# A memory-bound decode kernel: V of quad 14 in halves, a new order of the last V and wo, W_down in 128, 120 and 96 rows, fewer VectorE instructions, and 16 small loads of x

## The chip, the cores and the metric

The kernel runs on one core of a Trainium2 chip. The metric is the device time of one execution in microseconds (us). "Span" is the time from the first to the last instruction in the profile; it is about 2 us shorter than the time.

Names used below: the work on the K and V caches is done in 16 "quads" (0 to 15). A quad is four heads of one batch row: 8.39 MB of K and as many of V. "K15" is the K of quad 15, "V14" the V of quad 14. A load is spread over up to 16 DMA engines. The trace's landing records give the time at which each of them signalled that its share had landed; "the slowest engine" is the last of them, "the fastest" the first.

## The reference

The reference is a decode step: layer norm, attention over a cache of 8192 positions (2 batch rows, 32 heads of 128), a gated MLP, and two residuals.

```python
# A_x (2,1,512); k_cache, v_cache (2,32,8192,128); wq (512,4096); wo (4096,512)
# W_gate, W_up (512,1376); W_down (1376,512); all bf16
q = layernorm(x) @ wq
p = softmax(q @ k_cache^T * 128**-0.5)
h = x + (p @ v_cache) @ wo
n = layernorm(h)
gate = n @ W_gate;  gate = gate * (gate > 0)
out = h + (gate * (n @ W_up)) @ W_down
```

K and V together are 268 MB. Everything else is small beside that.

## The kernel before

K lands in a ring of two buffers, V in one buffer. VectorE multiplies K by q and folds it to scores, ScalarE takes the exponential, TensorE multiplies by V. All large loads are issued by SyncE (SP), in one order.

```python
    kring = ctx.enter_context(tc.tile_pool(name="kring", bufs=2))
    vring = ctx.enter_context(tc.tile_pool(name="vring", bufs=1))
# ... cut
    def lanes_of(o):
        osb = opool.tile([P, Dh], f32, tag="row", name="osb")
        nc.vector.tensor_scalar_mul(osb, o[:, 0:Dh], turn_of[:, 0:1])
        for t in range(1, TG):
            nc.vector.scalar_tensor_tensor(out=osb, in0=o[:, t * Dh:(t + 1) * Dh],
                                           scalar=turn_of[:, t:t + 1], in1=osb,
                                           op0=ALU.mult, op1=ALU.add)
        return osb
# ... cut
    for n in range(N - 1):                      # N = 16 quads
        scores(n, HALVES if n == 0 else (0, T))
        if n + 2 < N:
            load_k(n + 2)
        gather()
        collect()                               # lanes_of for a finished pair of quads
        if n + 2 < N:
            weighted_v(n)
            load_v(n + 1)                       # the single V buffer is free again
# ... cut
    load_wo(0)
    L = N - 1
    vts[L] = vts[L - 1]
    weighted_v(L - 1, 0, T // 2)
    load_part(vts[L], A_v_cache, L, 0, T // 2)
    weighted_v(L - 1, T // 2, T)
    CUTS = (T // 2, T * 7 // 8, T)
    for lo, hi in zip(CUTS[:-1], CUTS[1:]):
        load_part(vts[L], A_v_cache, L, lo, hi)
    for k in range(1, NGR):
        load_wo(k)
    scores(L)
# ... cut: W_gate and W_up are loaded, then W_down in 128, 128 and 88 rows of 4 KB
    attention_rows(0, NK - JG)                  # the wo rows that need no V15
    for lo, hi in zip(CUTS[:-1], CUTS[1:]):
        weighted_v(L, lo, hi)                   # second half of V15
    collect()
    gather()
    normalize(B - 1, NGR - 1)
    attention_rows(NK - JG, NK)                 # the last wo rows
# ... cut: layer norm, MLP, store
```

The softmax here doesn't subtract the row's maximum and nothing guards it: scores larger than these inputs give would overflow.

Of the kernel before, what the change touches and what calls it, by code (L numbers as in the profile page):

```python
# [7 lines left out]
ACT = mybir.ActivationFunctionType  # L8
ALU = mybir.AluOpType
AXIS = mybir.AxisListType  # L10


def _view(t, offset, dims):
    return bass.AP(tensor=t.tensor, offset=t.offset + offset, ap=[t.ap[0]] + list(dims))
# [3 lines left out]
def kernel(  # L18
# [13 lines left out]
    nc = tc.nc  # L32
    P = nc.NUM_PARTITIONS
    B, Sq, D = A_x.shape
    _, Hkv, Sk, Dh = A_k_cache.shape
    Hq = A_wq.shape[1] // Dh
    F = B_W_gate.shape[1]
# [37 lines left out]
    NG = T // TG  # L75
    pm = consts.tile([P, R + NG * W2], bf16)
    row_of = consts.tile([P, Q], f32)
    nc.vector.memset(eps_t, EPS)
    nc.vector.memset(mean_c, 1.0 / D)
    nc.vector.memset(zm, 0.0)  # L80
    nc.vector.memset(row_of, 0.0)
    ident = consts.tile([P, P], bf16)
    masks.make_identity(nc, ident)
    nc.gpsimd.memset(pm, 0.0)
# [11 lines left out]
    def build_masks():  # L96
        def red(out, in_, axis=AXIS.X):
            nc.vector.tensor_reduce(out=out, in_=in_, axis=axis, op=ALU.add)

        red(turn_of, ident.rearrange("p (g t h) -> p t g h", t=TG, h=G), AXIS.XY)  # L100
        red(lane_of, ident.rearrange("p (g u t h) -> p u h g t", u=2, t=TG, h=G), AXIS.XY)
        red(head_blk, ident.rearrange("p (h m) -> p h m", h=G))
        red(row_of[:, 0:B], ident.rearrange("p (g q) -> p q g", q=Q)[:, 0:B, :])
        red(pick, ident.rearrange("p (h m) -> p m h", m=M4))
        nc.vector.tensor_copy(spread, _view(lane_of, 0, [[G, 2], [1, G], [0, M4]]))
        nc.vector.tensor_copy(same, _view(head_blk, 0, [[0, NS], [1, G], [0, M4]]))

    ctx.enter_context(tc.manual_schedule(engines={ENG.PE, ENG.DVE, ENG.Activation, ENG.SP}))

# [31 lines left out]
    for c in range(KC):  # L141
# [6 lines left out]
    rstd = misc.tile([P, B], f32)  # L148
    nc.scalar.activation(out=rstd, in_=variance(xd, "ln1"), func=ACT.Sqrt, bias=eps_t, scale=1.0)
    nc.vector.reciprocal(out=rstd, in_=rstd)  # L150
    xn = misc.tile([P, KC, B], bf16)
    nc.vector.tensor_tensor(out=xn, in0=xd, in1=rstd.unsqueeze(1).to_broadcast([P, KC, B]),
                            op=ALU.mult)
    xnb = opool.tile([P, KC, B, Q], bf16, tag="row")
    nc.vector.tensor_copy(xnb, xn.unsqueeze(3).to_broadcast([P, KC, B, Q]))
    nc.scalar.activation(out=warm, in_=xn[0:1, 0, 0:1], func=ACT.Exp)
    build_masks()


# [39 lines left out]
    def load_v(n, cuts=(0, T)):  # L199
        vts[n] = vring.tile([P, T, Dh], bf16, tag="v", name="v")  # L200
        for lo, hi in zip(cuts[:-1], cuts[1:]):
            load_part(vts[n], A_v_cache, n, lo, hi)
# [4 lines left out]
    def scores(n, cuts=(0, T)):  # L207

        b, i = seq[n]
        kt = kts[n]  # L210
        sc = spool.tile([P, T], f32, tag="sc", name="sc")
        for lo, hi in zip(cuts[:-1], cuts[1:]):
            kp = kt[:, lo:hi, :]
            nc.vector.tensor_tensor(out=kp, in0=kp,  # L214
                                    in1=_view(qrep[:, b, i, :], 0, [[0, hi - lo], [1, Dh]]),
                                    op=ALU.mult)
            width = Dh
            while width > 8:
                half = width // 2
                nc.vector.tensor_tensor(out=kp[:, :, 0:half], in0=kp[:, :, 0:half],  # L220
                                        in1=kp[:, :, half:width], op=ALU.add)
                width = half
            nc.vector.tensor_reduce(out=sc[:, lo:hi], in_=kp[:, :, 0:8], axis=AXIS.X, op=ALU.add)  # L223
        for h in range(G):
            ps = slice(h * Q, (h + 1) * Q)
            nc.scalar.activation(out=p_of[ps, :, :, h],  # L226
                                 in_=sc[ps, :].rearrange("p (g t) -> p g t", t=TG), func=ACT.Exp,
                                 accum_out=zm[ps, b, i:i + 1],
                                 scale=SCALE)
# [19 lines left out]

    def lanes_of(o):  # L250

        osb = opool.tile([P, Dh], f32, tag="row", name="osb")
        nc.vector.tensor_scalar_mul(osb, o[:, 0:Dh], turn_of[:, 0:1])  # L253
        for t in range(1, TG):
            nc.vector.scalar_tensor_tensor(out=osb, in0=o[:, t * Dh:(t + 1) * Dh],  # L255
                                           scalar=turn_of[:, t:t + 1], in1=osb,
                                           op0=ALU.mult, op1=ALU.add)
        return osb

    def lane(n):  # L260
# [51 lines left out]
    def normalize(b, k):  # L312
        g = b * NGR + k
        nc.vector.tensor_scalar_mul(oc[:, k * JG:(k + 1) * JG, b], ou[:, b, k], zi[:, g:g + 1])

    HALVES = (0, T // 2, T)
    load_k(0, HALVES)
    load_k(1)
    load_v(0)
    for n in range(N - 1):  # L320
        scores(n, HALVES if n == 0 else (0, T))
        if n + 2 < N:
            load_k(n + 2)
        gather()
        collect()
        if n + 2 < N:
            weighted_v(n)
            load_v(n + 1)


    W = kring.tile([P, RING], bf16, tag="k", name="W")
# [5 lines left out]
            out=wo_sb[:, k * JG:(k + 1) * JG, :].rearrange("p k n -> p (k n)"),  # L337
            in_=A_wo[r0:r0 + NS * G * Dh, :].rearrange("(p j) n -> p (j n)", p=P))

    load_wo(0)  # L340
    L = N - 1
    vts[L] = vts[L - 1]
    weighted_v(L - 1, 0, T // 2)
    load_part(vts[L], A_v_cache, L, 0, T // 2)
    weighted_v(L - 1, T // 2, T)
    CUTS = (T // 2, T * 7 // 8, T)
    for lo, hi in zip(CUTS[:-1], CUTS[1:]):
        load_part(vts[L], A_v_cache, L, lo, hi)
    for k in range(1, NGR):
        load_wo(k)  # L350

    scores(L)
# [4 lines left out]
    RD = 4  # L357
    MT = RD * P
    FT = (F + MT - 1) // MT
    offs = [min(j * MT, F - MT) for j in range(FT)]  # L360
    wd_sb = X[:, 2 * KC * F:2 * KC * F + FT * RD * D].rearrange("p (j r n) -> p j r n", r=RD, n=D)
    skip = ((FT - 1) * MT - offs[-1]) // RD
    assert F % RD == 0 and F >= MT
    if skip:
        nc.gpsimd.memset(wd_sb[0:skip, FT - 1], 0.0)  # L365
    for g, w, c0, c1 in ((0, B_W_gate, 0, KC), (1, B_W_up, 0, KC - 1), (1, B_W_up, KC - 1, KC)):
        nc.sync.dma_start(out=wgu[:, g, c0:c1].rearrange("p c n -> p (c n)"),
                          in_=w.rearrange("(p c) n -> p (c n)", c=KC)[:, c0 * F:c1 * F])
    for j in range(FT):
        p0 = skip if j == FT - 1 else 0  # L370
        rows = B_W_down[j * MT:min((j + 1) * MT, F), :].rearrange("(p r) n -> p r n", r=RD)
        for r0, r1 in ((0, RD),) if j < FT - 1 else ((0, RD - 1), (RD - 1, RD)):
            nc.sync.dma_start(out=wd_sb[p0:, j, r0:r1], in_=rows[:, r0:r1])

    invert_z()
    weighted_v(L, 0, CUTS[0])
    for b in range(B):
        normalize(b, 0)
        if b < B - 1:
            for k in range(1, NGR):  # L380
                normalize(b, k)

    ar_ps = ps_mm.tile([P, D], f32, tag="mm")
    nc.tensor.matmul(out=ar_ps, lhsT=ident[0:B, :], rhs=x_row, start=True, stop=False,
# [6 lines left out]
                             start=False, stop=(k + P // Q >= NK), skip_group_check=True)  # L391

    attention_rows(0, NK - JG)
    for lo, hi in zip(CUTS[:-1], CUTS[1:]):
        weighted_v(L, lo, hi)
    collect()
    gather()
# [6 lines left out]
    for c in range(KC):  # L404
        nc.tensor.matmul(out=h_ps[:, c, :], lhsT=ar.rearrange("p (m c) -> p c m", c=KC)[:, c, :],  # L405
                         rhs=row_of[:, 0:B], start=(c == 0), stop=True, skip_group_check=True)
    hc = misc.tile([P, KC, B], f32)
    nc.vector.tensor_copy(hc, h_ps)  # L408
    mu = centred(hc, "ln2")
    NR = Q // B  # L410
    hd = opool.tile([P, KC, NR, B], bf16, tag="hd")
    nc.vector.tensor_tensor(out=hd, in0=_view(hc, 0, [[B, KC], [0, NR], [1, B]]),
# [92 lines left out]
```

## Time and profile before

| | before |
|---|---|
| time, median of 3 runs (range) | 663.25 us (662.31 to 663.41) |
| span of the profiled execution | 661.5 us |
| SP's DMA queue, share of 16 engines' span | 98.7% |
| VectorE busy | 604.7 us (91%) |

The first fence has lines of the profile page of before: its head, the busy time of each engine, the rows of DMA busy share and of GB/s in 40 equal slices of the span, the queue of the SP loads (packets, MB, and the time that they took as a share of 16 engines' span), and the sums of the chain of work that ended last.

```profile
span 661.5 us, 2931 instructions
...
PE 117.5 (18%) x1211; PEld 51.3 (8%) x1211; DVE 604.7 (91%) x188; ACT 55.8 (8%) x142; POOL 4.3 (1%) x8
...
DMA  9999999999999999999999999999999999999896
GB/s 381 444 444 444 429 396 444 440 440 441 440 396 440 440 437 444 436 404 441 432 440 444 436 409 440 432 436 444 433 416 440 428 433 444 440 416 440 356 426 242
...
q1 hardware_dynamic: 6398, 281.06, 98.7%
...
DMA 75%; PE 15%; another core or an unknown queue 8%; DVE 1%; ACT 0%; issue 0%; SPq 0%; DVEq 0%
```

The DMA row is at 9 (90% busy or more) until three slices before the end, and the chain that ended last is DMA for 75% of the span. This kernel is bound by the stream of K and V. In the trace's landing records, each 8.39 MB K or V lands 19.36 us after the one before it, which is 433 GB/s. VectorE at 91% is close behind, but a line of the list of waits (what waits for what: idle time in all, count, longest) shows that it waits for K, 13.7 us in all, so it does not set the pace:

```profile
DVE k L214 <- DMA k<-in_A_k_cache_dram: 13.7, 10, 2.3
```

The next fence has the first line of SyncE's own waits: what released an issue, the idle time in all, how often, and the longest. It is the wait of one load for an earlier one; the lines after it are waits for VectorE and TensorE to free a buffer.

```profile
SPq L192 <- DMA v<-in_A_v_cache_dram: 286.6, 15, 21.3
```

SP waits all the time, and that is harmless: when it ends, the engines still have an earlier load to work on. The next fence shows that for the end of the stream. It is the timeline of SP: start, duration, what was issued.

```profile
582.02 0.33 SPq L192 DMA_DIRECT2D v<-in_A_v_cache_dram  x1
...
618.44 2.14 SPq L192 DMA_DIRECT2D v<-in_A_v_cache_dram  x3
```

V14 is issued at 582.02 us, but K15, which was issued before it, has not landed on its last engine until 595.46 us. So V14 has a lead of 13.4 us: for that long it sits in the queues behind K15, and when K15 is done the engines go on without a break. V14 lands at 612.79 to 614.83 us (fastest and slowest engine), V15 in three parts until 640.99, the second half of wo at 645.90 on the slowest engine.

The windows below are two-microsecond stretches of before around the point where K15 is done. The columns are the stretch, its length, busy time (and instruction count) of PE, PEld, DVE, ACT and POOL, the granted TensorE clock, the DMA share and the GB/s.

```profile
594.00:596.00 2.00, 0.66 (x2) 0.29 (x2) 1.05 (x3) 1.94 (x5) 0.00 (x0) 0.50 1.14 492
596.00:598.00 2.00, 0.00 (x0) 0.10 (x1) 2.00 (x1) 0.28 (x2) 0.00 (x0) 0.50 0.98 426
```

The DMA share stays at 0.9 or more (it can read above 1; take that as full).

The last fence is the line of the timeline where the last wo rows start. A bracket in the timeline is the idle time before the instruction and what ended it.

```profile
645.94 1.88 PE L390 MATMUL ar_ps<-W,oc 128*2 128x512 bf16 x16 [1.89 <-DMA W<-in_A_wo_dram]
```

The last wo rows start 0.04 us after the last wo has landed. From there 15.6 us of a serial chain (wo rows, layer norm, MLP, store) lead to the end.

### The profile page before, as it was taken

Reading aid. Unit: us, or ns where it says so; the run is one execution under the profiler, and the core shown is the slowest. Engines: PE = TensorE matmul, PEld = TensorE weight load, DVE = VectorE, ACT = ScalarE, POOL = GpSimd, SP = SyncE. Lnnn points to the kernel's source line nnn. Section 1 sums busy time; section 2 is a strip of 40 time slices with the busy share of each in tenths; the row PEclk is TensorE's granted clock in tenths of the full one; section 3 lists DMA queues with packets and bytes.
Section 4 is the critical chain, followed back from the end, with each engine's and each line's share of the span. In section 5 each row is a group of like instructions: output and inputs, shape, how many; then the busy total and the mean of one; then the engine's idle time right before and its main releaser. Section 6 shows DMA issues by size and latency. Waiting matters only on the chain.

```text
span 661.5 us, 2931 instructions
## 1 busy us (share of the span) xinstructions
PE 117.5 (18%) x1211; PEld 51.3 (8%) x1211; DVE 604.7 (91%) x188; ACT 55.8 (8%) x142; POOL 4.3 (1%) x8
## 2 busy tenths in 40 slices
PE   2100302003030210303021030301103030120346
PEld 1000101001010000101000010100001010000113
DVE  2899999999999999999899998999899998999932
ACT  2201000010101010010101001010100101010010
POOL 1000000000000000000000000000000000000010
PEclk9755755657565565755556575555657555565766
DMA  9999999999999999999999999999999999999896
GB/s 381 444 444 444 429 396 444 440 440 441 440 396 440 440 437 444 436 404 441 432 440 444 436 409 440 432 436 444 433 416 440 428 433 444 440 416 440 356 426 242
DMA packets 6423, 281.24 MB, mean 425 GB/s; under 512 B 728, under 2 KB 818, under 8 KB 1290
## 3 DMA queue, kind: packets, MB, share of 16 engines
q1 hardware_dynamic: 6398, 281.06, 98.7%
q8 instruction: 9, 0.15, 0.1%
q14 instruction: 4, 0.03, 0.0%
q10 hardware_dynamic: 12, 0.00, 0.0%
HBM read 281.05 MB, written 0.00 MB: 425 GB/s over the span
## 4 chain that ended last, share of the span: by engine, by line
DMA 75%; PE 15%; another core or an unknown queue 8%; DVE 1%; ACT 0%; issue 0%; SPq 0%; DVEq 0%
DMA v<-in_A_v_cache_dram 69%; PE o L244 13%; DMA W<-in_A_wo_dram 4%; DMA wq_sb<-in_A_wq_dram 2%; PE qps L168 0%; DVE qrep L181 0%; PE h_ps L405 0%; PE ar_ps L390 0%; ACT qrep L179 0%; PE gate_ps L438 0%; PE up_ps L438 0%; PE y_ps L428 0%; DVE act L456 0%; ACT ar L401 0%
## 5 line engine op out<-in xcount | busy, mean ns | idle before, releaser
L214 DVE TENSOR_TENSOR k<-k,qrep 128x32768 bf16<-128x32768 bf16 (+1 forms) x17 | 275.7, 16217 | 13.7 <-DMA k<-in_A_k_cache_dram 13.7
L220 DVE TENSOR_TENSOR k<-k 128x16384 bf16<-128x16384 bf16 (+3 forms) x68 | 266.7, 3923 | 2.3
L244 PE MATMUL o<-v,pm 128*32 128x512 bf16 x1024 | 93.6, 545 | 410.4 <-DMA v<-in_A_v_cache_dram 410.4
L226 ACT ACTIVATE pm<-sc 32x256 bf16<-32x256 f32 x64 | 47.2, 737 | 564.5 <-DVE sc L223 528.2
L244 PEld LDWEIGHTS <-pm 128*32 128x32 bf16 x1024 | 39.3, 130 | 463.2 <-issue 289.4
L223 DVE TENSOR_REDUCE sc<-k 128x256 f32<-128x2048 bf16 (+1 forms) x17 | 36.7, 2161 | 1.6
L284 PE MATMUL rep<-osb,spread 128*64 128x128 f32 x16 | 5.2, 423 | 97.4 <-DVE osb L255 97.4
L226 ACT ACTIVATION_READ_ACCUMULATOR pm<-sc 32x1 f32 x64 | 15.0, 234 | 0.0
L181 DVE CAST qrep<-qps 32x512 bf16<-32x512 f32 x8 | 5.5, 692 | 8.1 <-ACT qrep L179 8.1
L284 PEld LDWEIGHTS rep<-osb,spread 128*64 128x64 f32 x16 | 2.2, 198 | 101.3 <-DVE osb L255 61.9
L255 DVE SCALAR_TENSOR_TENSOR osb<-o,turn_of,osb 128x128 f32<-128x128 f32 x24 | 8.4, 351 | 0.8
L253 DVE TENSOR_SCALAR osb<-o,turn_of 128x128 f32<-128x128 f32 x8 | 2.8, 344 | 5.2 <-PE o L244 5.2
L168 PE MATMUL qps<-wq_sb,xnb 128*64 128x512 bf16 x32 | 5.8, 507 | 7.1 <-DMA wq_sb<-in_A_wq_dram 5.1
L365 POOL MEMSET X<- 40x2048 bf16 x1 | 1.8, 1797 | 628.9 <-DVE sc L223 628.9
L179 ACT ACTIVATE qrep<-qps 32x512 bf16<-32x512 f32 x8 | 4.7, 586 | 8.2 <-PE qps L168 4.7
L408 DVE COPY hc<-h_ps 128x8 f32<-128x8 f32 x1 | 0.2, 166 | 5.6 <-PE h_ps L405 5.6
L145 DVE COPY xc<-x_ps 128x8 f32<-128x8 f32 x1 | 0.2, 168 | 4.7 <-PE x_ps L142 4.7
L307 DVE TENSOR_TENSOR zs<-zb,head_blk 128x16 f32<-128x16 f32 x1 | 0.2, 176 | 3.8 <-PE zb L304 3.8
L304 PE MATMUL zb<-zm,same 128*128 128x16 f32 x2 | 0.6, 386 | 14.9 <-ACT pm L226 14.9
L390 PE MATMUL ar_ps<-W,oc 128*2 128x512 bf16 x32 | 2.9, 499 | 1.9 <-DMA W<-in_A_wo_dram 1.9
L168 PEld LDWEIGHTS <-xnb 128*64 128x64 bf16 x32 | 2.5, 135 | 10.0 <-issue 5.1
L405 PE MATMUL h_ps<-row_of,ar 128*128 128x2 f32 x8 | 2.0, 375 | 0.7 <-ACT ar L401 0.7
(71 smaller groups left out, 32.4 us busy)
## 6 DMA issues: line engine op xcount, KB each, us to landing
k<-in_A_k_cache_dram SPq DMA_DIRECT2D x2, 4096.0 KB, 26.2
wq_sb<-in_A_wq_dram SPq DMA_DIRECT2D x1, 4096.0 KB, 12.3
W<-in_A_wo_dram SPq DMA_DIRECT2D x2, 2048.0 KB, 26.5
v<-in_A_v_cache_dram SPq DMA_DIRECT2D x1, 4096.0 KB, 12.0
v<-in_A_v_cache_dram SPq DMA_DIRECT2D x1, 3072.0 KB
X<-in_B_W_gate_dram SPq DMA_DIRECT2D x1, 1376.0 KB
X<-in_B_W_up_dram SPq DMA_DIRECT2D x1, 1032.0 KB, 19.5
v<-in_A_v_cache_dram SPq DMA_DIRECT2D x1, 1024.0 KB
```

The costliest lines, as they stand in the source:

```text
L168: nc.tensor.matmul(out=qps[h * B * Q:(h + 1) * B * Q], lhsT=xnb[:, c].rearrange("p b q -> p (b q)"), rhs=wq_v[:, c, g:g + QP, h0 + h, :], ...
L179: nc.scalar.activation(out=dst, in_=src, func=ACT.Copy)
L181: nc.vector.tensor_copy(dst, src)
L214: nc.vector.tensor_tensor(out=kp, in0=kp, in1=_view(qrep[:, b, i, :], 0, [[0, hi - lo], [1, Dh]]), op=ALU.mult)
L220: nc.vector.tensor_tensor(out=kp[:, :, 0:half], in0=kp[:, :, 0:half], in1=kp[:, :, half:width], op=ALU.add)
L223: nc.vector.tensor_reduce(out=sc[:, lo:hi], in_=kp[:, :, 0:8], axis=AXIS.X, op=ALU.add)
L226: nc.scalar.activation(out=p_of[ps, :, :, h], in_=sc[ps, :].rearrange("p (g t) -> p g t", t=TG), func=ACT.Exp, accum_out=zm[ps, b, i:i + 1 ...
L244: nc.tensor.matmul(out=o[g:g + W2], lhsT=_view(pm, (0 if lane else R) + t // TG * W2, [[1, W2]]), rhs=vt[:, t:t + TG, :].rearrange("p t d ...
L253: nc.vector.tensor_scalar_mul(osb, o[:, 0:Dh], turn_of[:, 0:1])
L255: nc.vector.scalar_tensor_tensor(out=osb, in0=o[:, t * Dh:(t + 1) * Dh], scalar=turn_of[:, t:t + 1], in1=osb, op0=ALU.mult, op1=ALU.add)
L284: nc.tensor.matmul(out=state["rep"][u * m:(u + 1) * m, :], lhsT=spread.rearrange("k u h m -> k (u h m)"), rhs=osb, start=True, stop=True, ...
L390: nc.tensor.matmul(out=ar_ps[g:g + B], lhsT=oc[:, k, :], rhs=wo_sb[:, k, :], start=False, stop=(k + P // Q >= NK), skip_group_check=True)
```

## The change

The change has five parts.

1. V14 is loaded in halves, so that the first half of V15 can follow as soon as TensorE has read the first half of V14. The last V follows V14 directly, and both halves of wo come after it.
2. W_down is loaded in 128, 120 and 96 rows instead of 128, 128 and 88.
3. Fewer VectorE instructions: `lanes_of` does one multiply and one reduce in place of four operations; small copies and memsets are merged or moved to GpSimd or ScalarE.
4. Scores are reduced once, not by part.
5. In quad 14, 16 small loads of x are issued from ScalarE's queue, of 1 to 16 rows of 16 bytes. Nothing reads what they land.

The diff, cut to what the argument touches:

```diff
     def lanes_of(o):
-        osb = opool.tile([P, Dh], f32, tag="row", name="osb")
-        nc.vector.tensor_scalar_mul(osb, o[:, 0:Dh], turn_of[:, 0:1])
-        for t in range(1, TG):
-            nc.vector.scalar_tensor_tensor(out=osb, in0=o[:, t * Dh:(t + 1) * Dh],
-                                           scalar=turn_of[:, t:t + 1], in1=osb,
-                                           op0=ALU.mult, op1=ALU.add)
+        om = opool.tile([P, TG * Dh], f32, tag="row", name="om")
+        nc.vector.tensor_tensor(out=om.rearrange("p (t d) -> p t d", d=Dh),
+                                in0=o.rearrange("p (t d) -> p t d", d=Dh),
+                                in1=_view(turn_of, 0, [[1, TG], [0, Dh]]), op=ALU.mult)
+        osb = opool.tile([P, Dh], f32, tag="osb", name="osb")
+        nc.vector.tensor_reduce(out=osb, in_=om.rearrange("p (t d) -> p d t", d=Dh), axis=AXIS.X,
+                                op=ALU.add)
         return osb
@@ the loop over quads
         gather()
+        if n == N - 2:
+            probe = consts.tile([16, 16, 8], bf16)
+            for j in range(1, 17):
+                nc.scalar.dma_start(out=probe[0:j, j - 1, :],
+                                    in_=A_x[0, 0, 0:8 * j].rearrange("(j n) -> j n", n=8))
         collect()
         if n + 2 < N:
             weighted_v(n)
-            load_v(n + 1)
+            load_v(n + 1, (0, T) if n + 3 < N else HALVES)
@@ after the loop
-    load_wo(0)
     L = N - 1
     vts[L] = vts[L - 1]
-    weighted_v(L - 1, 0, T // 2)
-    load_part(vts[L], A_v_cache, L, 0, T // 2)
-    weighted_v(L - 1, T // 2, T)
-    CUTS = (T // 2, T * 7 // 8, T)
-    for lo, hi in zip(CUTS[:-1], CUTS[1:]):
-        load_part(vts[L], A_v_cache, L, lo, hi)
-    for k in range(1, NGR):
+    CUTS = (0, T // 2, T * 7 // 8, T)
+    for lo, hi in zip(HALVES[:-1], HALVES[1:]):
+        weighted_v(L - 1, lo, hi)
+        for a, b in zip(CUTS[:-1], CUTS[1:]):
+            if lo <= a < hi:
+                load_part(vts[L], A_v_cache, L, a, b)
+    for k in range(NGR):
         load_wo(k)
@@ W_down
-    offs = [min(j * MT, F - MT) for j in range(FT)]
+    ROWS = (P, 120, F // RD - P - 120)
+    ends = [RD * sum(ROWS[:j + 1]) for j in range(FT)]
+    offs = [e - MT for e in ends]
# ... cut: memsets, copies, normalize_row, hc
```

Note two things. In the source, `load_v(14)` stands in the pass for quad 13, before the loads of x. And `attention_rows(0, NK - JG)` still stands ahead of the second half of V15 in TensorE's order, although wo now lands after V15.

More of the change, by code (lines that the diff above doesn't have):

```diff
@@ L77 @@
     row_of = consts.tile([P, Q], f32)
-    nc.vector.memset(eps_t, EPS)
-    nc.vector.memset(mean_c, 1.0 / D)
-    nc.vector.memset(zm, 0.0)
-    nc.vector.memset(row_of, 0.0)
+    nc.gpsimd.memset(eps_t, EPS)
+    nc.gpsimd.memset(mean_c, 1.0 / D)
+    nc.gpsimd.memset(zm, 0.0)
+    nc.gpsimd.memset(row_of, 0.0)
     ident = consts.tile([P, P], bf16)
@@ L104, in build_masks @@
         red(pick, ident.rearrange("p (h m) -> p m h", m=M4))
-        nc.vector.tensor_copy(spread, _view(lane_of, 0, [[G, 2], [1, G], [0, M4]]))
-        nc.vector.tensor_copy(same, _view(head_blk, 0, [[0, NS], [1, G], [0, M4]]))
+        nc.gpsimd.tensor_copy(spread, _view(lane_of, 0, [[G, 2], [1, G], [0, M4]]))
+        nc.gpsimd.tensor_copy(same, _view(head_blk, 0, [[0, NS], [1, G], [0, M4]]))
     ctx.enter_context(tc.manual_schedule(engines={ENG.PE, ENG.DVE, ENG.Activation, ENG.SP}))
@@ L150 @@
     nc.vector.reciprocal(out=rstd, in_=rstd)
-    xn = misc.tile([P, KC, B], bf16)
-    nc.vector.tensor_tensor(out=xn, in0=xd, in1=rstd.unsqueeze(1).to_broadcast([P, KC, B]),
-                            op=ALU.mult)
     xnb = opool.tile([P, KC, B, Q], bf16, tag="row")
-    nc.vector.tensor_copy(xnb, xn.unsqueeze(3).to_broadcast([P, KC, B, Q]))
-    nc.scalar.activation(out=warm, in_=xn[0:1, 0, 0:1], func=ACT.Exp)
+    nc.vector.tensor_tensor(out=xnb, in0=_view(xd, 0, [[B, KC], [1, B], [0, Q]]),
+                            in1=_view(rstd, 0, [[0, KC], [1, B], [0, Q]]), op=ALU.mult)
+    nc.scalar.activation(out=warm, in_=xnb[0:1, 0, 0, 0:1], func=ACT.Exp)
     build_masks()
@@ L222, in scores @@
                 width = half
-            nc.vector.tensor_reduce(out=sc[:, lo:hi], in_=kp[:, :, 0:8], axis=AXIS.X, op=ALU.add)
+        nc.vector.tensor_reduce(out=sc, in_=kt[:, :, 0:8], axis=AXIS.X, op=ALU.add)
         for h in range(G):
@@ L314, in normalize, with normalize_row @@
         nc.vector.tensor_scalar_mul(oc[:, k * JG:(k + 1) * JG, b], ou[:, b, k], zi[:, g:g + 1])
+    def normalize_row(b):
+        nc.vector.tensor_tensor(out=oc[:, :, b].rearrange("p (k j) -> p k j", j=JG), in0=ou[:, b],
+                                in1=_view(zi, b * NGR, [[1, NGR], [0, JG]]), op=ALU.mult)
     HALVES = (0, T // 2, T)
@@ L359 @@
     FT = (F + MT - 1) // MT
-    offs = [min(j * MT, F - MT) for j in range(FT)]
+    ROWS = (P, 120, F // RD - P - 120)
+    ends = [RD * sum(ROWS[:j + 1]) for j in range(FT)]
+    offs = [e - MT for e in ends]
     wd_sb = X[:, 2 * KC * F:2 * KC * F + FT * RD * D].rearrange("p (j r n) -> p j r n", r=RD, n=D)
-    skip = ((FT - 1) * MT - offs[-1]) // RD
-    assert F % RD == 0 and F >= MT
-    if skip:
-        nc.gpsimd.memset(wd_sb[0:skip, FT - 1], 0.0)
+    assert F % RD == 0 and sum(ROWS) * RD == F and len(ROWS) == FT and max(ROWS) <= P
+    for j in range(FT):
+        if ROWS[j] < P:
+            nc.gpsimd.memset(wd_sb[0:P - ROWS[j], j], 0.0)
     for g, w, c0, c1 in ((0, B_W_gate, 0, KC), (1, B_W_up, 0, KC - 1), (1, B_W_up, KC - 1, KC)):
@@ L369 @@
     for j in range(FT):
-        p0 = skip if j == FT - 1 else 0
-        rows = B_W_down[j * MT:min((j + 1) * MT, F), :].rearrange("(p r) n -> p r n", r=RD)
+        rows = B_W_down[ends[j] - RD * ROWS[j]:ends[j], :].rearrange("(p r) n -> p r n", r=RD)
         for r0, r1 in ((0, RD),) if j < FT - 1 else ((0, RD - 1), (RD - 1, RD)):
-            nc.sync.dma_start(out=wd_sb[p0:, j, r0:r1], in_=rows[:, r0:r1])
+            nc.sync.dma_start(out=wd_sb[P - ROWS[j]:, j, r0:r1], in_=rows[:, r0:r1])
     invert_z()
-    weighted_v(L, 0, CUTS[0])
-    for b in range(B):
-        normalize(b, 0)
-        if b < B - 1:
-            for k in range(1, NGR):
-                normalize(b, k)
+    weighted_v(L, 0, CUTS[1])
+    for b in range(B - 1):
+        normalize_row(b)
+    for k in range(NGR - 1):
+        normalize(B - 1, k)
     ar_ps = ps_mm.tile([P, D], f32, tag="mm")
@@ L393 @@
     attention_rows(0, NK - JG)
-    for lo, hi in zip(CUTS[:-1], CUTS[1:]):
+    for lo, hi in zip(CUTS[1:-1], CUTS[2:]):
         weighted_v(L, lo, hi)
@@ L406 @@
                          rhs=row_of[:, 0:B], start=(c == 0), stop=True, skip_group_check=True)
+    mu = centred(h_ps, "ln2")
     hc = misc.tile([P, KC, B], f32)
-    nc.vector.tensor_copy(hc, h_ps)
-    mu = centred(hc, "ln2")
+    nc.scalar.activation(out=hc, in_=h_ps, func=ACT.Copy)
     NR = Q // B
```

## The prediction

> **What bounds it now.** Page, DMA queues: the SP queue's packets take 98.7% of 16 engines' span. The chain that ended last is 75% DMA. In the trace's landing records every 8.39 MB K or V lands 19.36 us after the one before (433 GB/s); K of quad 15 lands at 595.46 us, V of quad 14 at 614.83, the last wo half at 645.90. VectorE is 91% busy but still waits for K (13.7 us in all). So stream time is critical until 645.90; after that come 15.6 us of a serial chain.
>
> **What the change is meant to win.** Before, V15's first half is issued at 618.44, only after PE has used all of V14; the engines go idle about 1 us (slowest engine) to 2.6 us (fastest). Halves remove that: about 1 us. W_down in 88 rows lands on 11 engines (12 semaphore updates recorded, against 16 for a 128-row load); the Trainium skill, "DMA: Bandwidth & Descriptors", "Why a DMA increments its semaphore by 16 and not by 1", says the engine count is the largest divisor up to 16. The busiest engine falls from 24 to 22 rows of 4 KB: 0.3 us, estimated from 1.2 us per 8 rows. VectorE: hc's copy leaves the chain (0.2 us); four 0.35 us operations become two of about 0.68 (estimate from the 96x512 multiply, 0.68 us): 0.1 us. The rest costs nothing now.
>
> **What it adds.** The 16 loads of x sit on ACT between quad 14's and quad 15's exponentials, and they take the same eight DMA semaphores in turn. V14's first half is numbered after them: it waits until load 9 has landed (second half: load 10). Before, it was issued at 582.02. Now it can't go before quad 14's exponentials are dispatched (595.6). Eight loads at 0.6 us each (x_row's issue 0.55, the store's 0.61) put load 9 at 600.4; about 2 us to land: 602.3. Issue to first bytes is 2.3 us (V15's first half: 618.44 to 630.43 with 9.68 of transfer). The stream restarts at about 604.6, not 595.46: a hole of 9 us, all on the critical path.
>
> Afterwards: V14 lands whole at 624, V15 at 643.4, wo at 648.2 and 653.1. A second cost: PE's order still puts the first 16 wo rows before V15's second half, and wo now lands after V15. So from 648.2: rows 1.9 us, V 2.5, lanes and gather 2.9, last rows start at about 655.5 (before 645.94), 2.4 us after their wo. Less 0.2, plus 0.4 for one lagging engine, and 15.5 of chain: span 671.2; with the 1.75 between span and time, about 672.8 us.
>
> **Prediction.** 672.8 us, 669.0 to 676.2. Faster by over 2%: 0.02; within 2%: 0.90; slower: 0.08.
>
> **What would show it.** DMA share: near zero between about 596 and 604, in one 16.5 us slice of the page. SP's waits: V's issue waiting for ACT-issued loads, about 20 us. V14's halves landing near 614 and 624. The critical chain going through the x loads, then PE's wait for wo, then V15's matmuls. No idle DMA between V14 and V15. Up to 595 nothing moves.
>
> **What would make it wrong.** ACT issues small loads at 0.3 us or lands them in 1 us: 2 to 3 us less. Landing takes 4 us as x_row did at the start: 2 to 3 more. PE at a faster granted clock: 1 us less. If the semaphores don't gate V14, about 661 to 663.

A semaphore is a counter that a load raises when it lands and that a later instruction waits for. The page and the views don't print the eight semaphores; the trace's landing records keep the number of the semaphore that each load signalled. Each load issued by SP or ScalarE signals one of eight, handed out in turn across both queues. A load that takes a semaphore waits until its previous user has landed. In the changed kernel, V14's halves come right after the 16 loads of x in that turn: in the records of after, V14's first half signals the same semaphore as loads 1 and 9, its second half the same as loads 2 and 10.

## The result and the profile after

The changed kernel took 670.92 us, median of 4 runs (670.11 to 671.89), against 663.24 us, median of 4 runs of before. The ratio is 1.0119 (95% interval 1.0102 to 1.0137): slower, by less than 2%. Here and below, a ratio is the mean time of one kernel's fast runs over that of the other's of the same rounds, so it is not quite the ratio of the medians quoted.

Lines of the page of after, as of before:

```profile
span 668.2 us, 2933 instructions
...
PE 119.9 (18%) x1211; PEld 52.2 (8%) x1211; DVE 606.2 (91%) x162; ACT 56.1 (8%) x143; POOL 6.7 (1%) x15
...
DMA  9999999999999999999999999999999999969995
GB/s 377 439 439 439 436 439 439 439 435 401 424 439 436 436 435 436 439 439 433 432 412 435 439 433 432 435 435 436 435 439 428 420 440 435 424 271 433 421 422 173
...
q1 hardware_dynamic: 6559, 281.06, 97.9%
...
q10 hardware_dynamic: 284, 0.01, 0.0%
...
DVE 61%; DMA 35%; PE 2%; ACT 1%; issue 0%; DVEq 0%
```

The 36th slice stands out: DMA digit 6, and 271 GB/s where its neighbours have 424 and 433. Queue q10 holds the loads of ScalarE's queue, so the 16 loads of x: 0.01 MB, 0.0% of the engines' time. By busy time they cost nothing. The sums of the chain do not point to them either: the chain has moved to VectorE (61%), because it is traced back through SP's wait into VectorE's work. What points to them is the list of SP's own waits:

```profile
SPq L190 <- DMA v<-in_A_v_cache_dram: 261.6, 15, 21.3
...
SPq L190 <- DMA probe<-in_A_x_dram: 43.1, 1, 43.1
```

The second of these lines is new. An issue of V waited for a load of x to land. The 43.1 us are counted from SP's previous issue at 554 us, so most of them are the ordinary wait for a buffer. When it ended shows in the timeline of ScalarE's queue and SP:

```profile
593.70 0.54 ACTq L331 DMA_DIRECT2D probe<-in_A_x_dram  x2
...
595.94 3.54 ACTq L331 DMA_DIRECT2D probe<-in_A_x_dram  x9
...
597.60 0.80 SPq L190 DMA_DIRECT2D v<-in_A_v_cache_dram  x2
```

V14 is issued at 597.60 us, 15.6 us later than before (582.02) and after K15 has landed (595.09 on the slowest engine). Load 9 was issued at 596.28 and landed at 597.55, 0.05 us before V14's issue. The Trainium skill, "DMA: Bandwidth & Descriptors", section "Anatomy of one DMA — SWDGE (gpsimd) path", notes that DMA engines do not wait on semaphores: a wait happens on the issuing sequencer. The trace agrees: the wait is SP's, and the 16 DMA engines were idle meanwhile, as these windows of after show (columns as above):

```profile
594.00:596.00 2.00, 0.66 (x2) 0.29 (x2) 1.35 (x2) 1.91 (x6) 0.00 (x0) 0.50 0.01 0
596.00:598.00 2.00, 0.00 (x0) 0.10 (x1) 2.00 (x1) 0.00 (x0) 0.00 (x0) 0.50 0.02 0
598.00:600.00 2.00, 0.00 (x0) 0.00 (x0) 2.00 (x1) 0.00 (x0) 0.00 (x0) 0.50 0.90 262
```

The DMA share is 0.01 and 0.02 where before had 1.14 and 0.98. V14's first half lands at 609.34 to 609.82. With 9.68 us of transfer for half a V, that is as if it had begun, at full pace, at about 599.7 to 600.1. (The packet records have its first packets at 598.55 to 599.29 on the 16 engines; these took 1.2 to 2.1 us each, the following ones 1.21. So the third window already reads 0.90, at 262 GB/s.) Counted in this way from K15's landing (593.19 to 595.09), the stream lost 5.0 us on the slowest engine and 6.5 us on the fastest. Below, this loss is called the hole.

The end of the kernel, in lines of the timeline of TensorE and VectorE:

```profile
645.67 1.87 PE L397 MATMUL ar_ps<-W,oc 128*2 128x512 bf16 x16 [6.59 <-DMA W<-in_A_wo_dram]
...
647.33 2.60 PE L242 MATMUL o<-v,pm 128*32 128x512 bf16 x32
...
650.00 0.69 DVE L251 TENSOR_TENSOR om<-o,turn_of 128x512 f32<-128x512 f32 x1 [13.65 <-PE o L242]
650.72 1.02 DVE L255 TENSOR_REDUCE osb<-om 128x128 f32<-128x512 f32 x1
...
653.22 1.88 PE L397 MATMUL ar_ps<-W,oc 128*2 128x512 bf16 x16 [0.99 <-DVE oc L313]
```

The last wo lands at 650.48, but its rows start only at 653.22. V15 had landed whole at 640.69, and still TensorE waited 6.59 us for the first half of wo, did those rows, and only then took V15's second half. Before, the rows started 0.04 us after the landing.

The landing times side by side (from the trace's landing records, slowest engine, us). "no loads" is the first experiment below.

| | before | after | no loads |
|---|---|---|---|
| K15 landed | 595.46 | 595.09 | 595.05 |
| V14 issued | 582.02 | 597.60 | 581.48 |
| V14 landed (halves after the change) | 614.83 | 609.82, 621.18 | 604.76, 614.48 |
| V15 landed, last part | 640.99 | 640.69 | 633.99 |
| wo, first half | 619.71 | 645.63 | 638.88 |
| wo, second half | 645.90 | 650.48 | 643.86 |
| last wo rows start | 645.94 | 653.22 | 644.96 |
| W_down landed, last part | 657.16 | 662.64 | 656.76 |

### The profile page after: what moved, and what is told of

Read it like the earlier page. It is cut to its first block, busy times and chain, and to the rows that moved or that the text cites. A ratio compares the mean times of both kernels' runs of the same rounds, so it can differ in the third digit from the quotient of the medians.

```text
span 668.2 us, 2933 instructions
## 1 busy us (share of the span) xinstructions
PE 119.9 (18%) x1211; PEld 52.2 (8%) x1211; DVE 606.2 (91%) x162; ACT 56.1 (8%) x143; POOL 6.7 (1%) x15
## 4 chain that ended last, share of the span: by engine, by line
DVE 61%; DMA 35%; PE 2%; ACT 1%; issue 0%; DVEq 0%
DMA k<-in_A_k_cache_dram 30%; DVE k L212 28%; DVE k L218 27%; DVE sc L221 3%; DMA W<-in_A_wo_dram 3%; DMA wq_sb<-in_A_wq_dram 2%; DVE qrep L179 1%; PE ar_ps L397 1%; DVE osb L255 0%; ACT qrep L177 0%; PE o L242 0%; PE h_ps L412 0%; DVE om L251 0%; PE qps L166 0%; PE gate_ps L445 0%
## 5 line engine op out<-in xcount | busy, mean ns | idle before, releaser
L242 PE MATMUL o<-v,pm 128*32 128x512 bf16 x1024 | 95.3, 551 | 410.9 <-DMA v<-in_A_v_cache_dram 410.9
L221 DVE TENSOR_REDUCE sc<-k 128x256 f32<-128x2048 bf16 x16 | 36.6, 2286 | 2.0 <-DVE k L218 0.5
L251 DVE TENSOR_TENSOR om<-o,turn_of 128x512 f32<-128x512 f32 x8 | 5.5, 683 | 13.7 <-PE o L242 13.6
L374 POOL MEMSET X<- 8x2048 bf16 (+1 forms) x2 | 3.5, 1794 | 621.6 <-DVE sc L221 621.6
L255 DVE TENSOR_REDUCE osb<-om 128x128 f32<-128x512 f32 x8 | 8.2, 1022 | 0.3
```

Source lines behind the costliest of these rows:

```text
L221: nc.vector.tensor_reduce(out=sc, in_=kt[:, :, 0:8], axis=AXIS.X, op=ALU.add)
L242: nc.tensor.matmul(out=o[g:g + W2], lhsT=_view(pm, (0 if lane else R) + t // TG * W2, [[1, W2]]), rhs=vt[:, t:t + TG, :].rearrange("p t d ...
L251: nc.vector.tensor_tensor(out=om.rearrange("p (t d) -> p t d", d=Dh), in0=o.rearrange("p (t d) -> p t d", d=Dh), in1=_view(turn_of, 0, [[1 ...
L255: nc.vector.tensor_reduce(out=osb, in_=om.rearrange("p (t d) -> p d t", d=Dh), axis=AXIS.X, op=ALU.add)
```

## The experiments

The theory: the loads of x cost all of the loss, because V14's issue must wait for one of them to have landed, and the stream stands idle. Rivals: the loads cost by their number or by what they move; the change of order of V15 and wo costs, not the loads; the tail has slack that hides a hole in the stream if it is early enough; the new W_down rows and VectorE operations gain or lose something of their own. Eleven kernels ran, each against before on the same chip. Each gave correct results.

### no_loads: the change without the 16 loads

```diff
         gather()
-        if n == N - 2:
-            probe = consts.tile([16, 16, 8], bf16)
-            for j in range(1, 17):
-                nc.scalar.dma_start(...)
         collect()
```

> The changed kernel without the 16 loads of x; everything else of the change stays. Theory 1 (the loads hold V of quad 14 back through the shared DMA semaphores): V14 is issued near 582 us again, its halves land near 605 and 615 us, the DMA queues never empty between 593 and 600 us, wo lands near 639 and 644 to 645 us, and the time is 662.0 to 664.0 us (before 663.2). Rival A (the cost is the new order, wo behind V15 while PE still takes the first wo rows before the second half of V15): the time stays near 669 to 671 us.

Measured: 662.49 us against 663.33 of before, ratio 0.9987 (0.9975 to 1.0). The timeline shows V14 issued early again, in one group with the parts of V15, and the last wo rows 8.3 us earlier than in after:

```profile
581.48 36.77 SPq L190 DMA_DIRECT2D v<-in_A_v_cache_dram  x5
```

and, from the stretch at the end,

```profile
644.96 1.87 PE L392 MATMUL ar_ps<-W,oc 128*2 128x512 bf16 x16 [0.99 <-DVE oc L313]
```

The loads cost 670.92 − 662.49 = 8.4 us (8.8 us by the two ratios), more than the whole loss. All the rest of the change together is worth 0.8 us, and the interval reaches 1.0, no gain at all.

### loads_alone: before, with only the 16 loads added

```diff
         gather()
+        if n == N - 2:
+            probe = consts.tile([16, 16, 8], bf16)
+            for j in range(1, 17):
+                nc.scalar.dma_start(out=probe[0:j, j - 1, :],
+                                    in_=A_x[0, 0, 0:8 * j].rearrange("(j n) -> j n", n=8))
         collect()
```

> The kernel before plus the 16 loads of x at the same place, nothing else of the change. Theory 1: V14 (whole) is issued near 597.6 us instead of 582.0, after load 9 has landed, the stream stands still from about 595 to 600 us, V14 lands near 619 to 620 us instead of 614.8; the old bubble between V14 and V15 stays and grows a little because the engines restart in step: 667.5 to 670.5 us. Rival A (wo order): within 1 us of before, 663 to 664.5 us.

Measured: 668.97 us against 663.33, ratio 1.0084 (1.007 to 1.0099). V14, here whole, waits for the same thing:

```profile
597.99 0.33 SPq L192 DMA_DIRECT2D v<-in_A_v_cache_dram  x1
```

```profile
SPq L192 <- DMA probe<-in_A_x_dram: 43.1, 1, 43.1
```

The loads alone cost 5.6 us. With the rest of the change they cost 8.4. The difference is examined in loads_v_first. One point of the expectation failed: the old pause ahead of V15's first half did not grow but shrank. Landing times less 9.68 us of transfer give 1.0 to 2.6 us for it in before (after the first half of wo, landed at 617.68 to 619.71) and 0.3 to 1.1 us here.

### loads_pool: the same 16 loads from GpSimd's queue

If the cost were the loads' data, descriptors or issue, it would stay. If it is the semaphores that SP and ScalarE share, it goes: in the built program the loads from GpSimd use others. They are held back until quad 14's first exponential, so that they start at the same time as in after.

```diff
-                nc.scalar.dma_start(out=probe[0:j, j - 1, :],
+                nc.gpsimd.dma_start(out=probe[0:j, j - 1, :],
# ahead of the loop, to place them in time:
+            after = consts.tile([16, 1], f32)
+            nc.gpsimd.tensor_copy(after, zm[0:16, seq[n][0], seq[n][1]:seq[n][1] + 1])
+            nc.gpsimd.tensor_copy(probe.rearrange("p j n -> p (j n)"), after.to_broadcast([16, 128]))
```

> The changed kernel with the same 16 loads, same rows and bytes, at the same time (after quad 14's first exponential), but issued by GpSimd, whose loads take other semaphores, so that no K or V waits for them. Theory 1: as without the loads, 662.0 to 664.5 us, V14 issued near 582 us. Rival B (the loads themselves disturb the stream: 136 tiny rows share the 16 engines with it): the time stays at 668 to 671 us.

Measured: 663.24 us against 663.33, ratio 1.0 (0.9987 to 1.0012). Both lines are of its timeline:

```profile
581.76 36.92 SPq L190 DMA_DIRECT2D v<-in_A_v_cache_dram  x5
...
594.71 4.23 POOL L335 DMA_DIRECT2D probe<-in_A_x_dram  x8 [0.30 <-POOL probe L332]
```

The first eight loads are issued at the same place, V14 is not held back, and most of the loss is gone. In the landing records these loads signal eight other semaphores than those of SP and ScalarE. (The other eight are issued from 601.67 to 617.41, later than in after, each when an earlier load on its own semaphore has landed.) The loads are not quite free: no_loads, in the same rounds on the same chip, took 662.49 us, and its slowest run (662.93) is faster than the fastest run here (662.94). So about 0.8 us of the 8.4 may be what the loads move or GpSimd's extra copies; the rest is where the loads stand in the turn of semaphores.

### loads_8: loads 9 to 16 only

```diff
-            for j in range(1, 17):
+            for j in range(9, 17):
```

> The changed kernel with the last 8 of the 16 loads only (9 to 16 rows). V14's first half then waits for the first load instead of the ninth, the second half for the second. Theory 1: V14 is issued near 594.8 us instead of 597.6, so the stream restarts 2.8 us earlier: 667 to 669 us. Rival B (cost by rows: 100 of the 136 rows remain): about 669 us, only about 26 percent of the cost gone, so the two are close here; V14's issue time decides.

Measured: 668.08 us against 663.33, ratio 1.0075 (1.0062 to 1.0088). With eight loads, V14's halves take the semaphores of the first and second load, and V14 is issued right after the first has landed:

```profile
595.03 16.38 SPq L190 DMA_DIRECT2D v<-in_A_v_cache_dram  x3
```

Half of the loads still cost 5.6 us over no_loads, two thirds of the whole cost. That speaks against a cost per load; a cost per row (100 of the 136 rows are left) would have come near, and loads_4 decides that. V14's issue at 595.03 is only 2.6 us earlier than in after, and already 13.5 us later than in no_loads. Most of the harm is done by waiting for even the first load: ScalarE issues it only after work of quad 14, near the time when K15 is done, and so the lead that V14 had in the queues is used up.

### loads_4: loads 13 to 16 only

This is the sharper test: with four loads, V14's halves fall on semaphores whose previous users are V12 and K14, long landed.

```diff
-            for j in range(1, 17):
+            for j in range(13, 17):
```

> The changed kernel with only the last 4 of the 16 loads (13 to 16 rows, 58 of the 136 rows), at the same place and on ACT's own queue. With 4 loads V14's halves fall on the fifth and sixth semaphore, whose last users are V12 and K14, long landed. Theory 1: V14 is issued near 582 us, no hole, 662.0 to 663.3 us, as without loads. A cost per load or per row (4 of 16, 58 of 136, of the 8.4 us between with and without) would give 664.6 to 666.1 us.

Measured: 662.66 us against 662.99, ratio 0.9998 (0.9984 to 1.0012). Timeline and windows of loads_4:

```profile
581.89 36.78 SPq L190 DMA_DIRECT2D v<-in_A_v_cache_dram  x5
...
593.79 0.74 ACTq L331 DMA_DIRECT2D probe<-in_A_x_dram  x2
```

```profile
594.00:596.00 2.00, 0.66 (x2) 0.29 (x2) 1.34 (x2) 1.95 (x6) 0.00 (x0) 0.50 1.18 508
596.00:598.00 2.00, 0.00 (x0) 0.10 (x1) 2.00 (x1) 0.06 (x2) 0.00 (x0) 0.50 0.92 393
```

V14 goes at 581.89 though the four loads are on the same ScalarE queue at the same time, and the stream has no hole (1.18 and 0.92 against 0.01 and 0.02 in after). Four loads cost nothing that shows (the interval overlaps that of no_loads) and eight cost 5.6 us. Of the causes considered here, only the place in the turn of eight explains both. The landing records confirm the place: in loads_4 V14's halves signal the semaphores of V12 and K14.

### loads_32: twice as many loads

```diff
-            probe = consts.tile([16, 16, 8], bf16)
-            for j in range(1, 17):
-                nc.scalar.dma_start(out=probe[0:j, j - 1, :],
-                                    in_=A_x[0, 0, 0:8 * j].rearrange("(j n) -> j n", n=8))
+            probe = consts.tile([16, 32, 4], bf16)
+            for i in range(32):
+                j = i % 16 + 1
+                nc.scalar.dma_start(out=probe[0:j, i, :],
+                                    in_=A_x[0, 0, 0:4 * j].rearrange("(j n) -> j n", n=4))
```

> The changed kernel with 32 loads of x instead of 16 (1 to 16 rows twice, 8 bytes a row instead of 16). V14's first half now waits for load 24, which the ACT queue issues about 5.3 us after load 9 (0.36 us each). Theory 1: V14 issued near 603 us instead of 597.6, the stream restarts near 605, time 675.5 to 677.5 us (changed kernel 670.9). Rival D (the loss is a fixed loss of lead: V14 is merely no longer queued ahead, whatever the number of loads): 670 to 672 us.

Measured: 675.89 us against 663.25, ratio 1.019 (1.0177 to 1.0204), on the edge of 2%. The time came out near what was expected, but the way there was wrong, and two errors cancelled. The expectation had V14's first half wait for load 24. In the built program and in the trace it waits for load 16, which landed at 600.65 (in the turn it stands between loads 23 and 24); V14's first half was issued at 600.70. Its second half waits for load 25, and that load landed only at 612.87, behind the packets of V14's first half (landed at 612.75 on the same engines). So the second half was issued at 612.88, when no part of V was left in the queues: a second hole, 12.9 us between the halves' landings in place of 9.68.

```profile
600.70 28.61 SPq L190 DMA_DIRECT2D v<-in_A_v_cache_dram  x5
```

```profile
SPq L190 <- DMA probe<-in_A_x_dram: 57.9, 2, 46.1
```

SP now waits twice for loads of x (2 in the count, against 1 in after). The Trainium skill, "DMA: Bandwidth & Descriptors", section "Issuing engines are not separate DMA queues", says that loads from all issuing engines run on the same 16 DMA engines and interleave. The traces agree: in after the first 12 loads of x, issued before V14, landed in 1.15 to 1.38 us, but load 16 took 10.9 us (599.04 to 609.93) behind V14's first half. Here a small load was fast only while the engines were free.

### loads_quad6: the 16 loads in quad 6 instead of quad 14

A rival held that a hole in the middle of the stream could be won back, since VectorE and TensorE have slack.

```diff
-        if n == N - 2:
+        if n == 6:
```

> The changed kernel with its 16 loads moved from quad 14 to quad 6, in the middle of the stream; V7 is then numbered after them. Theory 1: the hole is as wide there (V7 issued near 287.8 us instead of 271.8, engines still from about 285 to 290) and nothing later wins it back, because the DMA queues are full to the end: 4.4 to 6.5 us over the kernel without the loads, 667 to 669 us. Rival C (the two K buffers ahead absorb a hole in mid-stream, only one at the end costs): 662 to 664 us.

Measured: 670.34 us against 663.25, ratio 1.0106 (1.0092 to 1.012). V6 is issued at 288.47 us, 0.06 us after load 9 has landed, against 271.37 in no_loads. It lands at 310.03 to 310.58 against 302.81 to 304.79:

```profile
288.47 0.33 SPq L190 DMA_DIRECT2D v<-in_A_v_cache_dram  x1
```

(The expectation calls it V7.) The expectation of 667 to 669 us was missed by 1.3: the hole costs 7.9 us over no_loads, about as much as at quad 14, and is not won back over 350 us. On the slowest engine the difference even grows, from 5.8 us at V6 to 7.6 us at K15 (602.69 against 595.05): while the stream stood still the slow engines caught up with the fast ones, and fell behind them again later. The stream, busy all the time, had nothing to catch up with.

### v_first: without the loads, V15's second half ahead of the wo rows on TensorE

```diff
-    attention_rows(0, NK - JG)
     for lo, hi in zip(CUTS[1:-1], CUTS[2:]):
         weighted_v(L, lo, hi)
     collect()
+    attention_rows(0, NK - JG)
```

(On top of no_loads.)

> Without the loads, and PE takes the second half of V15 before the first 16 rows of wo. Without the loads PE sat until 638.9 us for wo though V15 had landed at 634.0, and the last 16 rows of wo started at 644.96, 1.1 us after their wo had landed. Expected: they start when wo has landed, about 644 us, but W_down's last rows (656.8 us) then end last: 661.5 to 662.4 us, 0.3 to 1.0 us under the kernel without loads. Rival E (the tail is set by W_down's landing alone): no difference, 662.5 us.

Measured: 663.30 us against 663.25, ratio 1.0001 (0.9988 to 1.0013). The wo rows were done 1.3 us earlier than in no_loads (ScalarE takes them at 645.59 against 646.88), but the end did not come earlier, and the expectation of 661.5 to 662.4 us was missed. One line of its waits says why (wait, total, count, longest):

```profile
PE y_ps L430 <- DMA X<-in_B_W_down_dram: 1.9, 3, 1.2
```

TensorE arrived earlier and then waited for W_down, which landed at 657.85. In this trace the end of the kernel is set by the stream again, and the order on TensorE is off the critical path.

### v_first_wd88: the same with W_down in 128, 128 and 88 rows

```diff
-    ROWS = (P, 120, F // RD - P - 120)
+    ROWS = (P, P, F // RD - 2 * P)
```

(On top of v_first.)

> As v_first, but W_down again in 128, 128 and 88 rows. My estimate was that 128, 120 and 96 rows bring W_down's end 0.3 us earlier; if it holds, this one is 0.1 to 0.4 us slower than v_first. But from W_up's landing to W_down's the median engine took 4.46 us in the kernel before, 4.77 with the loads alone (88 rows) and 5.1 to 5.6 us in the four traces with 120 and 96 rows: the alternative is that the new split is slower by about 0.6 us for the median engine and gains nothing for the slowest (4.3 to 5.1 against 4.3 to 4.5 us); then this one is equal or up to 0.5 us faster.

Measured: 662.57 us against 663.25, ratio 0.9989 (0.9975 to 1.0002). The intervals of this and of v_first overlap, but both carry the noise of before. The two kernels ran in the same rounds on the same chip, and compared directly no run of one reaches a run of the other (661.95 to 662.77 against 662.86 to 663.62): the old rows are faster, by 0.7 us in the medians. The landing records agree. From the landing of W_up to that of the last W_down, the median engine took 4.5 to 4.9 us in the four traces with 88 rows (before, loads_alone, v_first_wd88, v_first_wd88_fma) and 5.1 to 5.9 us in the nine with 96 rows; the slowest engine took 3.8 to 4.5 us against 4.3 to 5.8. Most of it lies between the first and the second part of W_down, that is with the 120 rows: 1.5 to 2.1 us against 2.4 to 2.9 on the median engine. So the new split loses time where a gain was intended.

### loads_v_first: the whole change, with V15's second half ahead of the wo rows

```diff
-    attention_rows(0, NK - JG)
     for lo, hi in zip(CUTS[1:-1], CUTS[2:]):
         weighted_v(L, lo, hi)
     collect()
+    attention_rows(0, NK - JG)
```

(On top of the changed kernel.)

> The changed kernel with its 16 loads, PE taking V15's second half before the first 16 rows of wo. In the changed kernel the last wo rows start 2.74 us after their wo has landed (653.22 against 650.48), because PE waits for the first half of wo (645.63) before V15's second half, landed at 640.69. Expected: they start when wo has landed, 2.5 to 2.7 us earlier; then W_down's landing (662.6 us) sets the end and 1.0 to 2.0 us are left: 668.9 to 670.0 us. If PE's order does not matter: 670.9 us.

Measured: 669.09 us against 662.99, ratio 1.0092 (1.0079 to 1.0106).

```profile
650.33 1.88 PE L397 MATMUL ar_ps<-W,oc 128*2 128x512 bf16 x16 [3.73 <-DMA W<-in_A_wo_dram]
```

The last wo rows now start 0.05 us after the last wo has landed (650.28), not 2.74 us after it. That is worth 1.8 us of the time (670.92 to 669.09). So of the 8.4 us, some 6.6 are the later landing of the last wo (643.86 to 650.48), and the rest is TensorE's order, which puts V15's second half behind the first wo rows: it starts the last rows 1.10 us after wo's landing in no_loads, and 2.74 us after it in after.

### v_first_wd88_fma: the old four VectorE operations put back as well

```diff
-        om = opool.tile([P, TG * Dh], f32, tag="row", name="om")
-        ...
+        osb = opool.tile([P, Dh], f32, tag="row", name="osb")
+        nc.vector.tensor_scalar_mul(osb, o[:, 0:Dh], turn_of[:, 0:1])
+        ...
```

(On top of v_first_wd88.)

> Candidate for the best version: no loads, V15 first on PE, W_down in 128, 128 and 88 rows, and the four-instruction sum over turns of the kernel before (1.5 us) instead of the two-instruction one (0.69 and 1.02 us in the trace of the changed kernel, 1.74 us with its gap). Off the critical path except once, at V15. Expected 662.2 to 662.9 us, no difference beyond 0.2 us from v_first_wd88, since W_down's landing sets the end.

Measured: 662.40 us against 662.99, ratio 0.9991 (0.9979 to 1.0004). The time does not tell the two forms apart, since VectorE is not what ends last there. The groups do (busy time and mean ns of one, then idle time before them). Two lines of before:

```profile
L255 DVE SCALAR_TENSOR_TENSOR osb<-o,turn_of,osb 128x128 f32<-128x128 f32 x24 | 8.4, 351 | 0.8
L253 DVE TENSOR_SCALAR osb<-o,turn_of 128x128 f32<-128x128 f32 x8 | 2.8, 344 | 5.2 <-PE o L244 5.2
```

And two of after:

```profile
L251 DVE TENSOR_TENSOR om<-o,turn_of 128x512 f32<-128x512 f32 x8 | 5.5, 683 | 13.7 <-PE o L242 13.6
...
L255 DVE TENSOR_REDUCE osb<-om 128x128 f32<-128x512 f32 x8 | 8.2, 1022 | 0.3
```

Four operations took 0.344 + 3 × 0.351 = 1.40 us, the two that replaced them 0.683 + 1.022 = 1.71 us. The whole of VectorE has 26 instructions fewer and is busy 1.5 us longer (606.2 against 604.7). The Trainium skill, "VectorE: DVE Perf Modes", section "Rules for kernel authors", advises to minimize the count of chained operations; here the trace differs, and the measurement decides. (The same table also calls `tensor_reduce` the slowest VectorE operation, and that is the form that was brought in.) By the shapes, the two operations go through 512 numbers a partition each, 1024 together, where the four went through 128 each, 512 together. The reduce also reads its 512 numbers with a step of 512 bytes between those that are added together. Which of the two makes it slow was not tried.

## Why the prediction was right or wrong

The time was predicted as 672.8 us (669.0 to 676.2) and measured as 670.92, within the range; "within 2%" was right as well. The mechanism was right, and several terms were off by more than the total shows.

| term | predicted | measured |
|---|---|---|
| first load of x issued | 595.6 | 593.70 |
| issue of one load of x | 0.6 us | 0.28 to 0.35 us (loads 1 to 9) |
| load 9 issued | 600.4 | 596.28 |
| load 9 from issue to landing | about 2 us | 1.27 us |
| V14's issue to its first bytes (landing less transfer, as the prediction worked it out) | 2.3 us | 2.1 to 2.5 us |
| stream restarts | 604.6 | about 600.1 (slowest engine) |
| hole in the stream | 9 us | 5.0 to 6.5 us |
| V15 landed | 643.4 | 640.69 |
| wo landed, second half | 653.1 | 650.48 |
| last wo rows after that | 2.4 us | 2.74 us |
| from there to the end of the span | 15.7 us | 15.0 us |
| from span to time | 1.75 us | 2.7 us (2.3 by the span in the run's record) |

- **The gate (the wait of V14 for a load of x) was right.** V14's first half waits for load 9, the second for load 10. It was a wait in the built program and not a property of the loads: loads_4 and loads_pool have no gate, and no loss against before; loads_8 has a gate and the loss.
- **The issue of load 9 was mis-sized, by 4.1 us.** This is the largest error. "Eight loads at 0.6 us each" was taken from single loads with other work around them; in a row, ScalarE issued one every 0.28 to 0.35 us, which is 2.2 us over eight. The other 1.9 us is the start: the first load went at 593.70, and the prediction had none before 595.6. With a faster landing, the stream came back 4.5 us earlier than predicted.
- **The lag was mis-sized the other way.** The prediction gave 0.4 us to a lagging engine. Counted from the restart at 600.1, V15 should have landed at 638.8 with two transfers of 19.36 us, and landed at 640.69: 1.9 us. Of that, 1.4 us is one engine, which landed V14's second half at 621.18 when the others had it by 619.77. The trace's packet records show a 16,384-byte block of the instruction queue about every 77 us until 542 us, and two more near the end, each one packet of 0.9 to 1.4 us. After several of them one more engine lands behind the others (by 1.3 us after the first, at 77.63). In after, one was fetched at 614.44. This is a coincidence in time in several places of the traces; no run took the fetches away, so it is not shown to be the cause. The Trainium skill, "Runtime: NRT & Kernel Launch", section "Instruction fetch mechanics", says such blocks are 16 KiB, as seen here, and that the cost of crossing a block boundary is mostly hidden. The page speaks there of the engine that executes; no run here shows whether it holds for a DMA engine that has no idle time to make it up.
- **The hole is critical: right.** The landing of the last wo moved by 6.6 us (no_loads to after), more than the hole's 5.0 to 6.5. Early in the kernel a hole costs as much (loads_quad6).
- **"The critical chain going through the x loads" was wrong as a reading.** The chain's sums went to 61% VectorE. The loads showed in SP's waits, with 43.1 us and not the 20 that the prediction named.
- **"Near zero between about 596 and 604" was too long and too late.** The windows show it from about 594 to 599, and it left one slice of the page at 271 GB/s.
- **The gain of the halves was there, and larger than "about 1 us".** They take away the pause ahead of V15: without the loads, the last wo lands at 643.86 against 645.90 before, of which 0.4 us was there already at K15. Yet the time gains 0.8 us at most (no_loads). In no_loads, TensorE's order starts the last rows 1.10 us after the landing. In v_first that order is undone and the gain still does not come, because there TensorE waits for W_down, which lands no earlier than before (657.85 against 657.16). With the old rows of W_down (v_first_wd88) it lands at 656.29.
- **0.3 us from W_down was wrong in sign.** With the old rows the kernel is 0.7 us faster (v_first_wd88 against v_first). Why the 120 and 96 rows take longer stays open. The Trainium skill, "DMA: Bandwidth & Descriptors", section "Why a DMA increments its semaphore by 16 and not by 1", gives the rule for how many engines a load uses; the landing records agree with it (the records show one update per engine, and one more where fewer than 16 take part: 12 for 88 rows, 16 for 120 rows on 15 engines, 16 for 96 and 128). The rule was right, and the step from fewer rows per engine to less time was not.
- **0.1 us from VectorE was wrong in sign.** "Two of about 0.68" was 0.683 for the multiply and 1.022 for the reduce. It cost 0.3 us where it is on the chain (650.00 to 651.74 in the timeline of after).

One point stays open: why V14 is numbered after the loads, though its call stands before them in the source. It was read in the built programs, and the landing records and the runs follow it, but no experiment changed it by itself. No run beat before beyond its interval; the nearest are no_loads (0.9987, to 1.0), v_first_wd88 (0.9989, to 1.0002) and v_first_wd88_fma (0.9991, to 1.0004).

## What to carry to other kernels

In a kernel bound by one stream of loads, ask of every added load not what it moves but what must now wait for it: small loads with 0.0% of the engines' time cost 8.4 us here, because a large load's issue had to wait for them and lost its lead in the queues. Read the issuing engine's own waits and windows of DMA share around the place; the busy table and the sums of the chain did not show it. And place loads that nobody waits for on a queue whose semaphores the stream doesn't use, or make sure that the large load's turn falls on an old one: the same loads from GpSimd cost about 0.8 us in place of 8.4, and four of them nothing that could be measured. Compare two variants with each other, and not only each with before: two differences of 0.7 to 0.8 us show here only in that way.

## What the Trainium skill lacked or had wrong

- "DMA: Bandwidth & Descriptors" has no word on loads of two issuing queues that draw on one set of semaphores: a large load then waits for small ones on the other queue. Here this cost 8.4 us (loads of x present or not) with 16 loads, 5.6 us with 8, nothing that shows with 4, and about 0.8 us from GpSimd.
- The same page gives no way to see why a W_down of 128, 120 and 96 rows, on 16, 15 and 16 engines, took the median engine 5.1 to 5.9 us, and one of 128, 128 and 88 rows, with 11 engines for the last part, 4.5 to 4.9 us.
- "VectorE: DVE Perf Modes" advises fewer operations in a chain. Here two took 1.71 us in place of 1.40 for four; the two go through 1024 numbers a partition and the four through 512. An fp32 reduce of 128x512 to 128x128 with strided reads took 1.02 us.
- "Runtime: NRT & Kernel Launch" says in "Instruction fetch mechanics" that the cost of crossing a block is mostly hidden, and doesn't speak of the DMA engine that brings the block. Here each 16 KiB block was one packet of 0.9 to 1.4 us, about every 77 us until 542 us, beside a stream that was busy all the time. That it delayed the stream is not shown.
